# One buffer of keys and queries divided into four, in a sparse-attention and soft mixture-of-experts kernel

## Chip, cores and metric

The kernel runs on one core of one Trainium2 chip. The metric is the device time of one execution in microseconds (us). Before the change three runs gave a median of 304.71 us (303.28 to 306.85).

## What is computed

Inputs are q, k and v of 8 batches, 8 heads, 576 tokens and 64 values a head, all float32. The attention is sparse, its result is the input of a soft mixture of experts (MoE):

```python
scores = scale * np.matmul(q, k.transpose(0, 1, 3, 2))
mask_local = (rel >= 0) & (rel < stride)                      # stride 32, heads 0 to 3
mask_strided = (rel >= 0) & (pos[None, :] % stride == pos[:, None] % stride)   # heads 4 to 7
attn = softmax(where(mask, scores, -1e9));  attn_out = attn @ v
...
logits = x @ phi                  # x: 4608 tokens x 512, 32 slots
d = softmax(logits, axis=0);  slot_input = d.T @ x
slot_out[e] = relu(slot_input[e] @ w1[e]) @ w2[e]             # 8 experts, 4 slots each
out = softmax(logits, axis=1) @ slot_out
```

## The kernel before

The attention works in 16 groups (`i` = 0 to 15). A group is two local heads and two strided heads of one batch, so two groups make a batch; "even" and "odd" below mean `i`. The work of a group is cut into some 50 named steps, and a table `PHASE` gives each step a due time within a group. A step of group `i` is due at 10 · i + PHASE, all steps of all groups are sorted by that, and each engine runs its instructions in the order in which they were written. Semaphore waits are put in by the layer that records the instructions: it keeps track of who wrote and read what part of which buffer.

The steps that matter here, in the order of the data:

- `D` (lines 240 to 242): SyncE (SP) starts the load of 512 tokens of keys or queries of two heads, 256 KB, into one of three places of 512 columns (`nat`). `kL`, `qL`, `kS`, `qS` are local keys, local queries, strided keys, strided queries.
- `Dt` (lines 244 to 247), in even groups: SP starts two loads of 128 KB, the first 64 tokens of keys and of queries of all 8 heads of the batch, into the place `tnat`.
- `g` (lines 270 to 272): GpSimd (POOL) sorts a loaded place into one of two others (`nat2`).
- `T` (line 279) and `Tt` (line 300): TensorE (PE) transposes a sorted place, or `tnat`, into a PSUM bank (line 277).
- `e` (lines 282 to 297) and `et` (line 302): ScalarE (ACT) copies a bank into the transposed keys or queries `kt` or, for the first tokens, into `tl`. Keys take two copies of 64 rows, queries one of 128 rows.
- `kc` (lines 307 to 316): POOL copies keys of the first tokens from `tl` into `kt`.
- `SL` and `SS` (lines 321 to 337): PE computes the scores, 36 small products (`score`, line 319). `SL` writes a bank that the copies `ekS` had just emptied.
- `a`, `m`, `b`, `s` on VectorE (DVE), `EX` on ACT: mask, maximum, subtraction, exponential, sum (lines 347 to 369). `P`, `f`, `AA`, `AL`, `AS`, `n`, `X`, `LG` follow: weights transposed, values applied (line 397), normalised, transposed, logits. Every fourth group adds the steps of the 64 first tokens of a batch pair, and odd groups add the slot sums.
- `Dv`, `C2` (lines 249 to 268) and `Ds` (lines 257 to 262): loads and sorting of the values. `Ds` waits until PE has used the strided values of the group before.

Weights of the experts, 512 KB a load, go on the same SP queue between these loads: 28 into buffers of their own, spread over the attention, and 14 more into buffers of the attention (`alias`, lines 178 to 187) as each falls free near its end. After the last group PE, DVE and ACT compute the experts and the output (from line 651).

All places of keys and queries (`nat`, `nat2`, `kt`, `tl`, `tnat`) are column ranges of one buffer `kqn` of 6,912 columns: three places of `nat` at columns 0 to 1535, two of `nat2` at 1536 to 2559, then `kt` with kL (1,152 columns), qL (512), kS (1,152) and qS (512) up to 5887, `tl` at 5888 to 6399 and `tnat` at 6400 to 6911.

Of the kernel before, what the change touches and what calls it, by code (L numbers as in the profile page):

```python
# [19 lines left out]
B, H, S, D = 8, 8, 576, 64  # L20
# [13 lines left out]
    Tt=7.4853, et=9.1043, kcL=10.5339, kcS=12.0504, gkL=2.4513, gqL=2.5317, TkL=6.2817, ekL=8.2205, gkS=6.6666,  # L34
# [3 lines left out]
    AL=29.4276, AA=27.8312, nA=34.2734, nL=31.3378, AS=29.6166, nS=31.6162, XS=32.1661, xS=32.38, XL=31.9169,  # L38
# [35 lines left out]
def tile_sparse_attention_soft_moe(  # L74
# [23 lines left out]
    def big(nm, cols, dt=F32):  # L98
        return const.tile([P, cols], dt, name=nm)
# [12 lines left out]


    KQ = ("kL", "qL", "kS", "qS")
    kqn = big("kqn", 6912)
    pb = big("pb", 1152)
    ptb = big("ptb", 1024)
    vb_ = big("vb", 4096)
# [6 lines left out]
    def nat(x, i):  # L125

        lo = 512 * ((4 * i + KQ.index(x) + 2) % 3)
        return kqn[:, lo:lo + 512]

    def nat2(x):  # L130

        lo = 1536 + 512 * (KQ.index(x) % 2)
        return kqn[:, lo:lo + 512]

    kt, lo = {}, 2560
    for x in KQ:
        n = 2 * S if x[0] == "k" else S - 64
        kt[x] = kqn[:, lo:lo + n]  # L140
        lo += n
    tl = kqn[:, 5888:6400].rearrange("p (j x t) -> p j x t", j=4, x=2)
    tnat = kqn[:, 6400:6912]

    psg = {1: pb[:, 0:640].rearrange("p (s k a) -> p s k a", s=5, a=2),
           2: pb[:, 640:1152].rearrange("p (s x) -> p s x", s=4)[:, :, 0:3 * NI].rearrange("p s (k a) -> p s k a", a=3)[:, :, :, 0:2]}
# [25 lines left out]
    def give(t):  # L172
# [2 lines left out]

    alias = [(("gqL", "gkS", "gqS"), kqn, 0), (("gqS", "TkS", "TqS"), kqn, 1), (("TqS", "SL", "SS"), kqn, 2),
             (("SL", "SS"), kqn, 3), (("SL", "SS"), kqn, 4), (("SL", "SS", "kcS", "Tt-"), kqn, 5), (("AL-", "AA-", "C2-"), vb_, 0), (("AL", "AA", "C2"), vb_, 1), (("AL", "AA"), vb_, 2), (("AL", "AA"), vb_, 3),
             (("AS",), vs, 0), (("AS",), vs, 1), (("AS", "AL"), ptb, 0), (("LG", "XB"), xtb, 0)]  # L180

    def last(x):
        return PER * (NQ - 1 - x.count("-")) + PHASE[x.strip("-")]

    alias = sorted(((max(last(x) for x in names) + .01, n, t[:, 1024 * k:1024 * k + 1024]) for n, (names, t, k) in enumerate(alias)),
                   key=lambda x: x[:2])
# [53 lines left out]
    def emit_D(x, i):  # L240
        src = (k if x[0] == "k" else q)[i // 2, heads(i, x[1]), 64:]
        nc.sync.dma_start(out=nat(x, i).rearrange("p (h x) -> p h x", h=2), in_=src.rearrange("h (p n) d -> p h (n d)", n=TN))
# [27 lines left out]
    def emit_g(x, i):  # L270

        PC(out=nat2(x).rearrange("p (n h d) -> p h n d", n=TN, h=2), in_=nat(x, i).rearrange("p (h n d) -> p h n d", n=TN, h=2))  # L272
# [6 lines left out]
    def emit_T(x, i):  # L279
        turn("T" + x, i, nat2(x))  # L280
# [647 lines left out]
```

## Time and profile before

| what | us |
|---|---|
| runs before, median (lowest to highest) | 304.71 (303.28 to 306.85) |
| the profiled execution, own time | 302.76 |
| its span, first to last instruction | 301.0 |
| busy PE / DVE / ACT / POOL in the span | 235.7 / 182.5 / 154.7 / 101.2 |
| mean granted TensorE clock in the span | 0.924 |

The rows of the trace come from this one execution. PE is matrix products and transposes, PEld the loading of their stationary operand, SPq the queue of SP. "L296" is line 296 of the kernel. A number behind "idle before" or in square brackets is the time in which the engine did nothing ahead of the instruction, with what ended it. The granted clock is told as a share: 1.0 is 2.4 GHz and 0.5 is 1.2 GHz.

### The profile page before, as it was taken

What the parts mean: (1) busy time and instruction counts of PE and PEld (TensorE: products, weight loads), DVE (VectorE), ACT (ScalarE), POOL (GpSimd) and SP (SyncE); (2) the same over time, 40 slices, a digit from 0 to 9 for tenths busy, and PEclk for the clock granted to TensorE, in tenths of its full rate; (3) what the DMA queues carried; (4) which work ended last, traced back from release to release, by engine and by line L of the source; (5) the groups of instructions that cost most, each with busy time, mean ns of one, the idle gap of its engine ahead of it and who ended that gap; (6) DMA issues with size and microseconds to landing.
All of it is one profiled execution on the core that took longest, in us unless ns stands there. A gap on an engine that the chain in (4) does not pass through costs nothing.

```text
span 301.0 us, 9638 instructions
## 1 busy us (share of the span) xinstructions
PE 235.7 (78%) x3901; PEld 182.2 (61%) x3901; DVE 182.5 (61%) x405; ACT 154.7 (51%) x325; POOL 101.2 (34%) x170
## 2 busy tenths in 40 slices
PE   5866984994997897799699499992868977799800
PEld 2755973994977786788689497971632322355700
DVE  5063881684589588468689368993241466834720
ACT  1537735874664973777596467861210014524610
POOL 5473651653338258063466252621000200000000
PEclk9997996999899999799999799997777999999975
DMA  7999689579658868839696956499836999818997
GB/s 215 302 277 293 201 252 251 186 200 276 199 135 287 271 189 237 270 113 287 184 287 174 318 176 194 136 289 298 280 116 211 330 357 348 277 54 304 310 350 242
DMA packets 80940, 72.79 MB, mean 242 GB/s; under 512 B 33280, under 2 KB 75648, under 8 KB 80896
## 3 DMA queue, kind: packets, MB, share of 16 engines
q1 hardware_dynamic: 79936, 71.84, 78.4%
q8 instruction: 31, 0.51, 0.7%
q10 hardware_dynamic: 960, 0.33, 0.6%
q14 instruction: 13, 0.11, 0.1%
HBM read 62.72 MB, written 9.44 MB: 240 GB/s over the span
## 4 chain that ended last, share of the span: by engine, by line
PE 51%; DMA 19%; DVE 10%; ACT 9%; SPq 2%; issue 2%; POOL 1%; DVEq 0%; ACTq 0%; POOLq 0%
DMA kqn<-in_q_dram 14%; PE bank L319 9%; PE bank L277 8%; PE bank L397 6%; ACT kqn L296 6%; PE bank L839 4%; PE bank L871 3%; PE bank L736 3%; PE bank L442 3%; PE bank L566 3%; PE bank L389 3%; DMA vs<-in_v_dram 3%; DMA wb<-in_moe_w_dram 2%; PE bank L461 2%; PE bank L472 2%
## 5 line engine op out<-in xcount | busy, mean ns | idle before, releaser
L296 ACT COPY kqn<-bank 64x512 f32<-64x512 f32 (+1 forms) x96 | 59.2, 617 | 49.9 <-DMA kqn<-in_q_dram 40.6
L272 POOL COPY kqn<-kqn 128x512 f32<-128x512 f32 x64 | 41.7, 669 | 87.9 <-PE bank L277 45.6
L319 PE MATMUL bank<-kqn 128*32 128x128 f32 (+1 forms) x1152 | 36.9, 284 | 27.1 <-ACT kqn L296 27.1
L319 PEld LDWEIGHTS bank<-kqn 128*32 128x32 f32 x1152 | 32.9, 125 | 33.0 <-issue 20.1
L277 PE MATMUL bank<-cf,kqn 128*128 128x128 f32 x288 | 42.5, 297 | 4.0 <-POOL kqn L272 4.0
L277 PEld LDWEIGHTS bank<-cf,kqn 128*128 128x128 f32 x288 | 35.2, 153 | 9.3 <-POOL kqn L272 6.2
L354 DVE TENSOR_TENSOR pb<-bank,cb 128x512 f32<-128x512 f32 (+2 forms) x48 | 22.7, 474 | 29.3 <-PE bank L319 10.7
L424 DVE TENSOR_TENSOR xnb<-bank,rz 128x512 f32<-128x512 f32 x32 | 21.6, 687 | 11.6 <-PE bank L397 8.3
L369 DVE TENSOR_REDUCE rz<-pb 128x10 f32<-128x640 f32 (+1 forms) x32 | 21.9, 683 | 10.8 <-ACT pb L366 10.7
L362 DVE TENSOR_TENSOR pb<-pb,mx 128x640 f32<-128x640 f32 (+1 forms) x32 | 28.0, 875 | 0.6
L397 PE MATMUL bank<-vs,ptb 128*32 128x128 f32 x512 | 18.7, 282 | 5.8 <-DMA vs<-in_v_dram 5.8
L359 DVE TENSOR_REDUCE mx<-pb 128x10 f32<-128x640 f32 (+1 forms) x32 | 22.0, 688 | 0.6
L366 ACT ACTIVATE pb<-pb 128x640 f32<-128x640 f32 (+1 forms) x32 | 19.7, 615 | 1.8 <-DVE pb L362 1.7
L389 PE MATMUL bank<-cf,pb 128*128 128x128 f32 x128 | 20.1, 281 | 0.5 <-ACT pb L366 0.3
L393 ACT COPY ptb<-bank 128x512 f32<-128x512 f32 x32 | 19.4, 606 | 0.8 <-PE bank L389 0.8
L267 POOL COPY vb<-vb 64x1024 f32<-64x1024 f32 x16 | 16.6, 1037 | 8.5 <-DMA vb<-in_v_dram 7.5
L397 PEld LDWEIGHTS bank<-vs,ptb 128*32 128x32 f32 x512 | 15.5, 113 | 6.1 <-issue 6.1
L397 PE MATMUL bank<-vb,ptb 128*32 128x128 f32 x512 | 18.0, 274 | 0.0
L442 PE MATMUL bank<-cf,xnb 128*128 128x128 f32 x128 | 17.9, 284 | 0.1
L268 POOL COPY vb<-vb 64x1024 f32<-64x1024 f32 x16 | 17.0, 1060 | 0.7
L389 PEld LDWEIGHTS bank<-cf,pb 128*128 128x128 f32 x128 | 15.2, 145 | 1.7 <-ACT pb L366 0.9
L442 PEld LDWEIGHTS bank<-cf,xnb 128*128 128x128 f32 x128 | 14.8, 145 | 1.2 <-DVE xnb L424 0.7
(143 smaller groups left out, 375.3 us busy)
## 6 DMA issues: line engine op xcount, KB each, us to landing
wb<-in_moe_w_dram SPq DMA_DIRECT2D x47, 512.0 KB
kqn<-in_k_dram SPq DMA_DIRECT2D x32, 256.0 KB
kqn<-in_q_dram SPq DMA_DIRECT2D x32, 256.0 KB
vb<-in_v_dram SPq DMA_DIRECT2D x32, 144.0 KB
vs<-in_v_dram SPq DMA_DIRECT2D x32, 128.0 KB
kqn<-in_moe_w_dram SPq DMA_DIRECT2D x6, 512.0 KB
out_dram<-kqn SPq DMA_DIRECT2D x5, 512.0 KB
vb<-in_moe_w_dram SPq DMA_DIRECT2D x4, 512.0 KB
```

The lines of the kernel that those rows point to most:

```text
L272: PC(out=nat2(x).rearrange("p (n h d) -> p h n d", n=TN, h=2), in_=nat(x, i).rearrange("p (h n d) -> p h n d", n=TN, h=2))
L277: nc.tensor.transpose(out=t[0][:, 128 * n:128 * n + 128], in_=src[:, 128 * n:128 * n + 128], identity=ident)
L296: ACT(out=dst, in_=src)
L319: nc.tensor.matmul(out=t[0][32 * c:32 * c + 32, x:x + wd], lhsT=lhsT, rhs=rhs, start=True, stop=True, skip_group_check=True)
L354: nc.vector.tensor_tensor(out=dst, in0=box[t, i][0][:, lo:lo + 2 * n * kk].rearrange("p (s k a) -> p s k a", s=n, a=2), in1=mk.rearrange(" ...
L359: nc.vector.tensor_reduce(out=part(box[i][0], w), in_=psg[w].rearrange("p s k a -> p s a k"), op=ALU.max, axis=AX.X)
L362: nc.vector.tensor_tensor(out=psg[w], in0=psg[w], in1=over(box[i][0], w), op=ALU.subtract)
L369: nc.vector.tensor_reduce(out=part(box[i][1], w), in_=psg[w].rearrange("p s k a -> p s a k"), op=ALU.add, axis=AX.X)
L389: nc.tensor.transpose(out=t[0][:, 128 * r:128 * r + 128], in_=pb[:, lo + 128 * r:lo + 128 * r + 128], identity=ident)
L397: nc.tensor.matmul(out=t[0][32 * c:32 * c + 32, 128 * r:128 * r + 128], lhsT=lhsT, rhs=rhs, start=True, stop=True, skip_group_check=True)
L424: nc.vector.tensor_tensor(out=xn[:, place(i, s)].rearrange("p r (a d) -> p r a d", a=2), in0=t[0].rearrange("p (r a d) -> p r a d", r=4, a=2),
L442: nc.tensor.transpose(out=t[0][:, 128 * r:128 * r + 128], in_=xn[:, place(i, s), r, :], identity=ident)
```

## The change

The buffer `kqn` becomes four: `natb` (the loaded and sorted places and `tnat`), `kLb` (local keys), `kSb` (strided keys) and `qtb` (both queries and `tl`). They have 3,072 + 1,152 + 1,152 + 1,536 = 6,912 columns together. The list `alias`, which gives parts of 1,024 columns to expert weights at the end of the attention, is written for the new buffers: six parts as before, but two now lie in `natb` beyond the first, and each has its own last users. No computation, size or due time is changed. From the line of the buffers on the numbers of lines move, at most by one behind line 176.

```diff
-    kqn = big("kqn", 6912)
+    natb = big("natb", 3072)
+    kLb, kSb = big("kLb", 2 * S), big("kSb", 2 * S)
+    qtb = big("qtb", 1536)
...
-        return kqn[:, lo:lo + 512]
+        return natb[:, lo:lo + 512]
...
-    kt, lo = {}, 2560
-    for x in KQ:
-        n = 2 * S if x[0] == "k" else S - 64
-        kt[x] = kqn[:, lo:lo + n]
-        lo += n
-    tl = kqn[:, 5888:6400].rearrange("p (j x t) -> p j x t", j=4, x=2)
-    tnat = kqn[:, 6400:6912]
+    kt = {"kL": kLb, "kS": kSb, "qL": qtb[:, 0:512], "qS": qtb[:, 512:1024]}
+    tl = qtb[:, 1024:1536].rearrange("p (j x t) -> p j x t", j=4, x=2)
+    tnat = natb[:, 2560:3072]
...
-    alias = [(("gqL", "gkS", "gqS"), kqn, 0), (("gqS", "TkS", "TqS"), kqn, 1), (("TqS", "SL", "SS"), kqn, 2),
-             (("SL", "SS"), kqn, 3), (("SL", "SS"), kqn, 4), (("SL", "SS", "kcS", "Tt-"), kqn, 5), (("AL-", "AA-", "C2-"), vb_, 0), (("AL", "AA", "C2"), vb_, 1), (("AL", "AA"), vb_, 2), (("AL", "AA"), vb_, 3),
+    alias = [(("gqL", "gkS", "gqS"), natb, 0), (("gqS", "TkS", "TqS"), natb, 1), (("TqS", "Tt-"), natb, 2),
+             (("SL", "SS"), kLb, 0), (("SL", "SS"), kSb, 0), (("SL", "SS"), qtb, 0),
+             (("AL-", "AA-", "C2-"), vb_, 0), (("AL", "AA", "C2"), vb_, 1), (("AL", "AA"), vb_, 2), (("AL", "AA"), vb_, 3),
```

What it does to the instructions is seen in the waits. On ACT the copies of group 5 stand like this before; the first two rows are the copies of its strided keys (`ekS`), the third of its strided queries. Names with HW are the semaphores of transfers, eight of which the SP queue uses in turn:

```order
L296 COPY kqn<-bank_120 64x16x32 [waits DMAHW0_49,DMAHW7_49,PE_49,Activation_49]
L296 COPY kqn<-bank_120 64x16x32 [waits Activation_49]
L296 COPY kqn<-bank_114 128x512 [waits PE_49,Activation_49]
L446 COPY xtb<-bank_115 128x512 [waits PE_49,Activation_49]
L452 COPY xtb<-bank_119 128x512 [waits DVE_49,PE_49]
```

The same place of the changed kernel:

```order
L295 COPY kSb<-bank_123 64x16x32 [waits PE_49,Activation_49]
L295 COPY kSb<-bank_123 64x16x32 [waits Activation_49]
L295 COPY qtb<-bank_117 128x512 [waits PE_49,Activation_49]
L445 COPY xtb<-bank_118 128x512 [waits PE_49,Activation_49]
L451 COPY xtb<-bank_122 128x512 [waits DVE_49,PE_49]
```

The first copy no longer waits for two transfers; nothing else moved. The two are the `Dt` loads of group 6, whose `tnat` lies in other columns than the strided keys. The same pair of waits goes from the `ekS` copies of groups 1, 3, 5, 7, 9, 11 and 13, and in group 0 from the copies of the local keys; group 15 has none.

On the SP queue the two `Dt` loads (line 247) of group 6 stand here before, between the loads of local queries and of strided keys:

```order
L242 DMA kqn<-in_q_dram 128x2x256 [waits DMAHW6_49,Pool_49]
L247 DMA kqn<-in_k_dram 64x8x64 [waits DMAHW7_49,Activation_49]
L247 DMA kqn<-in_q_dram 64x8x64 [waits DMAHW0_49]
L242 DMA kqn<-in_k_dram 128x2x256 [waits DMAHW1_49,Pool_49]
L261 DMA vs<-in_v_dram 32x1024 [waits DMAHW2_49,PE_49]
```

And in the changed kernel:

```order
L241 DMA natb<-in_q_dram 128x2x256 [waits DMAHW6_49,Pool_49]
L246 DMA natb<-in_k_dram 64x8x64 [waits DMAHW7_49]
L246 DMA natb<-in_q_dram 64x8x64 [waits DMAHW0_49]
L241 DMA natb<-in_k_dram 128x2x256 [waits DMAHW1_49,Pool_49]
L260 DMA vs<-in_v_dram 32x1024 [waits DMAHW2_49,PE_49]
```

The first `Dt` load no longer waits for a copy of ACT, in group 6 that of the local queries of group 5; in group 0 a wait for DVE goes, in group 2 it becomes one for PE, and the others lose theirs. The third place is the end of the attention on the SP queue. Before, one weight load stands ahead of the values `Dv` of group 15 (line 252) and four behind:

```order
L216 DMA kqn<-in_moe_w_dram 128x4x256 [waits DMAHW3_49,PE_49,Pool_49]
L252 DMA vb<-in_v_dram 64x9x64 [waits DMAHW4_49]
L252 DMA vb<-in_v_dram 64x9x64 [waits DMAHW5_49]
L216 DMA kqn<-in_moe_w_dram 128x4x256 [waits PE_49,DMAHW6_49,Activation_49,Pool_49]
L216 DMA kqn<-in_moe_w_dram 128x4x256 [waits DMAHW7_49,Activation_49]
```

After:

```order
L215 DMA natb<-in_moe_w_dram 128x4x256 [waits DMAHW3_49,PE_49,Pool_49]
L215 DMA natb<-in_moe_w_dram 128x4x256 [waits DMAHW4_49,PE_49]
L251 DMA vb<-in_v_dram 64x9x64 [waits DMAHW5_49]
L251 DMA vb<-in_v_dram 64x9x64 [waits DMAHW6_49]
L215 DMA kLb<-in_moe_w_dram 128x4x256 [waits PE_49,DMAHW7_49,Activation_49,Pool_49]
```

One weight load of 512 KB has moved ahead of the values. The order on PE, ACT, DVE and POOL is the same in both kernels.

## Rows read from the trace of the kernel before

**Rows 1.** The waits of all engines: who waited, for whom, us in total, times, longest.

```profile
ACT kqn L296 <- DMA kqn<-in_q_dram: 40.6, 8, 7.9
...
PE bank L319 <- ACT kqn L296: 27.1, 7, 5.6
```

**Rows 2.** Timeline around the wait of group 5: start, length, engine, instructions, idle time before.

```profile
66.14 0.75 ACT L366 ACTIVATE pb<-pb 128x640 f32<-128x640 f32 x1
66.89 1.09 PE L277 MATMUL bank<-cf,kqn 128*128 128x128 f32 x8
66.95 0.63 SPq L247 DMA_DIRECT2D kqn<-in_q_dram  x1
72.01 1.83 ACT L296 COPY kqn<-bank 64x512 f32<-64x512 f32 x3 [5.12 <-DMA kqn<-in_q_dram]
73.37 1.93 PE L319 MATMUL bank<-kqn 128*32 128x128 f32 x53 [3.96 <-ACT kqn L296]
```

**Rows 3.** The chain that ended last, in order of time: start, us, what.

```profile
41.40 6.64 DMA kqn<-in_q_dram
...
66.95 4.91 DMA kqn<-in_q_dram
```

**Rows 4.** Windows: length, busy PE, PEld, DVE, ACT, POOL (instructions), granted clock, DMA share, GB/s.

```profile
60.70:69.40 8.70, 8.70 (x202) 7.96 (x193) 7.78 (x15) 4.89 (x11) 5.02 (x9) 1.00 0.80 223
69.40:73.40 4.00, 0.04 (x5) 0.06 (x5) 1.42 (x4) 1.34 (x3) 1.22 (x2) 1.00 0.81 231
73.40:87.00 13.60, 13.60 (x240) 12.16 (x244) 8.91 (x21) 10.49 (x24) 5.51 (x10) 0.87 0.59 179
87.00:96.30 9.30, 9.27 (x199) 7.96 (x190) 8.07 (x17) 5.06 (x11) 4.92 (x9) 1.00 0.90 269
96.30:99.20 2.90, 0.01 (x2) 0.04 (x3) 1.30 (x4) 1.32 (x3) 1.17 (x2) 1.00 0.68 196
99.20:109.70 10.50, 10.50 (x226) 9.39 (x230) 7.87 (x17) 9.61 (x21) 6.28 (x10) 1.00 0.78 253
109.70:118.20 8.50, 8.48 (x197) 7.77 (x189) 8.34 (x17) 5.08 (x11) 5.01 (x10) 1.00 0.79 223
118.20:122.00 3.80, 0.00 (x0) 0.01 (x1) 1.45 (x4) 1.28 (x3) 1.22 (x2) 1.00 0.70 186
...
183.90:193.10 9.20, 9.20 (x199) 8.16 (x191) 7.98 (x17) 6.83 (x15) 4.86 (x8) 1.00 0.63 189
```

**Rows 5.** Longer windows of the attention, and one short one.

```profile
0.00:24.00 24.00, 16.18 (x160) 11.06 (x160) 9.72 (x18) 8.53 (x14) 14.20 (x27) 1.00 0.92 268
24.00:48.00 24.00, 18.40 (x370) 16.66 (x370) 15.29 (x30) 13.41 (x27) 11.71 (x20) 0.91 0.82 244
48.00:194.00 146.00, 127.12 (x2535) 113.67 (x2539) 105.42 (x223) 101.02 (x211) 70.17 (x118) 0.95 0.74 219
66.00:72.00 6.00, 3.41 (x57) 2.97 (x49) 4.37 (x7) 0.89 (x2) 4.15 (x8) 1.00 0.95 294
```

**Rows 6.** The SP queue's own waits.

```profile
SPq L247 <- DVE kqn L617: 1.6, 1, 1.6
```

**Rows 7.** Timeline of SP and POOL: loads of keys and queries and their sorting.

```profile
60.13 0.37 SPq L242 DMA_DIRECT2D kqn<-in_q_dram  x1
...
64.74 0.38 SPq L242 DMA_DIRECT2D kqn<-in_k_dram  x1
...
69.84 0.61 POOL L272 COPY kqn<-kqn 128x512 f32<-128x512 f32 x1 [0.64 <-DMA kqn<-in_k_dram]
...
71.48 0.38 SPq L242 DMA_DIRECT2D kqn<-in_q_dram  x1
```

**Rows 8.** Timeline of POOL and PE at the end of the attention.

```profile
200.52 1.03 POOL L267 COPY vb<-vb 64x1024 f32<-64x1024 f32 x1 [7.47 <-DMA vb<-in_v_dram]
...
203.68 1.06 PE L397 MATMUL bank<-vb,ptb 128*32 128x128 f32 x32
...
210.58 1.93 PE L397 MATMUL bank<-vs,ptb 128*32 128x128 f32 x32 [5.84 <-DMA vs<-in_v_dram]
```

More of the change, by code (lines that the diff above doesn't have):

```diff
@@ L127, in nat @@
         lo = 512 * ((4 * i + KQ.index(x) + 2) % 3)
-        return kqn[:, lo:lo + 512]
+        return natb[:, lo:lo + 512]
     def nat2(x):
         lo = 1536 + 512 * (KQ.index(x) % 2)
-        return kqn[:, lo:lo + 512]
-    kt, lo = {}, 2560
-    for x in KQ:
-        n = 2 * S if x[0] == "k" else S - 64
-        kt[x] = kqn[:, lo:lo + n]
-        lo += n
-    tl = kqn[:, 5888:6400].rearrange("p (j x t) -> p j x t", j=4, x=2)
-    tnat = kqn[:, 6400:6912]
+        return natb[:, lo:lo + 512]
+    kt = {"kL": kLb, "kS": kSb, "qL": qtb[:, 0:512], "qS": qtb[:, 512:1024]}
+    tl = qtb[:, 1024:1536].rearrange("p (j x t) -> p j x t", j=4, x=2)
+    tnat = natb[:, 2560:3072]
     psg = {1: pb[:, 0:640].rearrange("p (s k a) -> p s k a", s=5, a=2),
```

## The prediction

> **What bounds the kernel now.** I read the table of waits first, then the timeline around its longest entries, the chain that ended last, and windows cut at the ends of the waits. In the table the reader is to see one wait that leads to another: ACT stood 40.6 us in 8 waits before a copy of line 296, each until a load of queries had landed, and PE stood 27.1 us in 7 waits before the scores, line 319, until such a copy was done [rows 1]. The timeline shows one of them whole. In group 5 ACT was free at 66.89 (66.14 + 0.75). PE began the transposes of strided keys and queries there and ended them at 67.98. Yet the copy of the strided keys began at 72.01, after 5.12 us [rows 2]. What landed then was started at 66.95 by line 247, that is `Dt`, the first tokens of group 6: in the chain that load takes 4.91 us, to 71.86 [rows 2, 3]. The copy neither reads nor writes what it brings. PE could not begin the scores of group 5 before the copy had emptied their bank, and began at 73.37, after 3.96 us of idleness [rows 2].
>
> The windows show what the kernel is bound by apart from that. From 60.7 to 69.4 PE is busy for 8.70 of 8.70 us, then 0.04 of 4.00; from 73.4 to 87.0 all of 13.60; 9.27 of 9.30, then 0.01 of 2.90; 10.50 of 10.50; 8.48 of 8.50, then 0.00 of 3.80 [rows 4]. Between the waits PE leaves no gap, in them it does nothing, and this repeats every second group.
>
> **The change part by part.**
>
> *The wait of ACT for `Dt`.* It goes from the copies of groups 1, 3, 5, 7, 9, 11 and 13. What is late next is in group 5 the end of the transposes: the two copies of keys, 0.6 us each, can begin at about 67.5 and end at 68.7, and PE comes to the scores at 69.4. So PE's whole idle time goes: 7 waits, 27.1 us [rows 1]. The trace has a case without the wait. Group 15 has no `Dt` behind it, and the stretch 183.9 to 193.1 that leads to it took 9.20 us, where its like, 87.0 to 99.2, took 9.30 + 2.90 = 12.20 [rows 4]. The difference, 3.0 us, is the idle time. In group 0 the wait ended when PE's transposes ended as well, so I count nothing.
>
> *What DVE takes back.* In the waits DVE worked on: 1.42, 1.30 and 1.45 us [rows 4]. With the stretch before, it has 7.78 + 1.42 = 9.20 us of work where PE has 8.70, 9.37 where PE has 9.30, and 9.79 where PE has 8.50. That is 0.5, 0.07 and 1.3 us more, 0.6 in the mean, and the next copies hang on DVE's results through the exponential. Seven times 0.6 is 4.3 us back. The other groups have 8.91 of DVE in 13.60 and hide it [rows 4]. Bounds: 0 if DVE uses its slack there, 9 if all seven are like the third.
>
> *What the transfers take back.* The bytes stay, so the DMA engines must go faster. In the first 48 us they were busy 0.92 · 24 + 0.82 · 24 = 41.8 us [rows 5]. The best share that a row shows is 0.95 [rows 5]; at that, they need 44.0 us. PE's first two idle times lie there; the longest is 5.6 [rows 1], and with one like the others they are 9.5. Only 4 of these fit if every byte is wanted by then, so 5.5 come back; none do if the loads there run ahead of their use. I take 3, the middle. In the rest the share is 0.74 over 146 us, 108 us of work [rows 5]. Less the other five idle times, about 17.5 us, that is 108 in 128.5, a share of 0.84. I charge nothing for it, and the rival below does.
>
> *The clock.* The granted clock was 0.91 from 24 to 48 us and 0.95 from 48 to 194 [rows 5], 0.09 · 24 + 0.05 · 146 = 9.5 us of lost clock. It fell to half in some stretches that follow a wait: 0.87 from 73.4 to 87.0 after 4.0 us without products, but 1.00 from 99.2 to 109.7 after 2.9 [rows 4]. Without these waits between 0 and 9.5 us return. I take 3, since a faster PE then meets DVE, with 35.4 us of work in the four groups from 60.7 to 109.7 [rows 4].
>
> The Trainium skill, in TensorE: Matmul & The Clock Gate, section HAM oscillation, says that a wait for DMA in every round lets the clock fall, that the work behind it then starts at half speed, and that this costs the throttled time times one half. By that rule all of the 9.5 us would return. The trace agrees in one of the two cases above and not in the other.
>
> *The wait of SP ahead of `Dt`.* In group 0 it was for DVE, 1.6 us [rows 6]. The next loads go out that much earlier, but the DMA engines are at a share of 0.92 there [rows 5], so between 0 and 1.6 us is won; I take 1. The other seven held SP until ACT's copy of local queries. They go too, and the loads behind (strided keys, values) start earlier. Nothing of this costs time, and it is part of the slack that the transfers need.
>
> *The weight load ahead of `Dv` of group 15.* 512 KB at 294 GB/s [rows 5] are 1.8 us. The values come that much later, so POOL's sorting at 200.52 and PE's products at 203.68 too. They have cover: the next products wait until 210.58 for the other values, 5.84 us [rows 8], and the bytes ahead of those stay the same. I count nothing; without the cover it costs 1.8.
>
> *The rest.* No instruction is added or changed, and the four memsets of the key buffers stay four.
>
> The sum: -27.1 + 4.3 + 3 - 3 - 1 = -23.8 us. Against the profiled execution's own 302.76 that is 279.0. The median of the runs shown is 1.95 above it, so I predict 280.9 for the median. The term bounds give -27.1 - 9.5 - 1.6 = -38.2 on one side and -27.1 + 9 + 5.5 = -12.6 on the other.
>
> **The rivals.**
>
> *The loads become the bound.* A place for loaded keys is free only when POOL has sorted it, and SP stands until then. From the load of strided queries at 60.13 to the next at 71.48 is 11.35 us, and 5.1 of them lie between the start of a load at 64.74 and POOL's sorting at 69.84 [rows 7]. For it: the loads already take 4.9 and 6.6 us in the chain [rows 3], and at a higher share they would wait longer for each other. Against it: SP issued nearly without pause in that time, and from 99.2 to 109.7 PE ran without a gap at a share of 0.78 [rows 4]. If each group took 11.35 us, a pair would take 22.7, where four groups from 73.4 to 122.0 took 48.6, 24.3 a pair [rows 4]. Then 1.6 · 7 = 11 us are won: 293.5 to the median.
>
> *All of the clock returns, and DVE keeps up.* Then -27.1 + 2 + 1 - 8 - 1 = -33: 271.7. For it: PE has no gap between waits, so each microsecond at half speed shows in full. Against it: DVE has 8.34 us of work in a window of 8.50 [rows 4].
>
> *Slower: the end of the attention waits for transfers.* Its place is the wait for the last values, 210.58 [rows 8]. Until 194 us the transfers have 22.1 + 19.7 + 108.0 = 149.8 us of work [rows 5]. If they could not pass the mean share of 149.8 / 194 = 0.77, everything won would be spent again there. The moved weight load would add 1.8 us, and a half clock behind the longer wait what it cost from 73.4 to 87.0, 0.13 · 13.6 = 1.8 [rows 4]: 304.71 + 3.6 = 308.3. It decides from the point where the share cannot rise above 0.77; rows 5 show 0.92 over 24 us, so I think it unlikely.
>
> *The change does not do what it says.* The layer that records the instructions could have put other waits in their place. The order shows none in the attention, so this is as unlikely: 304.7.
>
> **How the numbers follow.** Forecast 0.60, the loads 0.17, the clock 0.19, slower 0.02, no effect 0.02. The forecast's own range is 275 to 288. The range reaches towards the two larger rivals, 270 to 293, and leaves some 0.15 out. A measurement of this kernel can tell about 1% from no change; 293.5 is still 3.7% faster, so faster has 0.96, within 1% 0.02, slower 0.02.
>
> **What would show it.** Right: the wait of ACT for the load of queries is gone from the table, and PE's idle time before line 319 is under 6 us in total; windows of odd groups last 8.5 to 10 us without an idle piece behind; the granted clock is 1.0 from 50 us to the end of the attention; the share of DMA in the attention is above 0.80; the time between the end of the attention and the end of the program has not changed by more than 2 us. The terms would be wrong if PE is idle before its transposes or POOL before line 272 until a load has landed (the loads), or if PE waits for DVE or ACT ahead of line 389 (DVE). The prediction is wrong if PE's idle time only moves to another line.

## The result, and the profile after

The changed kernel takes 277.34 us in the median of 4 executions (276.10 to 278.78), the kernel before 304.94 beside it: a ratio of 0.9095, 95% interval 0.9025 to 0.9165. Two more sessions, told among the experiments, gave 0.9179 and 0.9131. Ratios and intervals leave out executions that lie well above the fastest of their kernel; medians count all. The profiled execution took 277.12, with a span of 275.3 (before 302.76 and 301.0) and a mean granted clock of 0.942 (before 0.924).

The waits of the changed kernel, all engines and then PE's own: who waited, for whom, us in total, times, longest.

```profile
POOL natb L271 <- DMA natb<-in_q_dram: 23.5, 18, 4.1
POOL natb L271 <- DMA natb<-in_k_dram: 22.7, 15, 3.5
...
PE bank L276 <- POOL natb L271: 12.1, 12, 2.3
PE bank L396 <- DMA vs<-in_v_dram: 6.0, 3, 4.8
...
PE bank L276 <- DVE pb L361: 0.7, 1, 0.7
```

Both waits of [rows 1] are gone: no copy of ACT waits for a load, and PE has no wait before its scores (now line 318). In their place PE waits before its transposes (276) for POOL's sorting (271), and POOL for loaded keys and queries. From the first transposes to the last wait for values, at 181.5, one wait of PE is for DVE, of 0.7 us, and none for ACT. A part of the wait for POOL stood in the kernel before already:

```profile
PE bank L277 <- POOL kqn L272: 4.0, 5, 1.8
```

The timeline at the place of [rows 2], group 5:

```profile
60.31 1.09 PE L276 MATMUL bank<-cf,natb 128*128 128x128 f32 x8
...
61.05 1.30 ACT L295 COPY kSb<-bank 64x512 f32<-64x512 f32 x2 [0.77 <-PE bank L276]
...
62.75 1.18 PE L318 MATMUL bank<-kLb,qtb 128*32 128x128 f32 x34
```

The copies of strided keys now begin 0.74 us after PE began the transposes that feed them, where they began 5.12 us behind (72.01 against 66.89), and the scores have no idle time ahead (no bracket).

Three windows divide the span: up to the last wait for values, that wait, and the rest. The columns are those of [rows 4]. Before:

```profile
0.00:204.74 204.74, 172.07 (x3295) 149.57 (x3295) 140.86 (x296) 130.12 (x268) 98.27 (x167) 0.95 0.78 231
204.74:210.58 5.84, 0.00 (x1) 0.03 (x2) 1.03 (x3) 0.00 (x0) 1.06 (x1) 0.73 1.09 275
210.58:301.00 90.42, 63.61 (x606) 32.59 (x606) 40.57 (x107) 24.54 (x57) 1.84 (x2) 0.88 0.82 265
```

After:

```profile
0.00:181.52 181.52, 166.08 (x3295) 142.28 (x3295) 137.06 (x297) 131.17 (x268) 96.65 (x168) 0.97 0.90 261
181.52:186.63 5.11, 0.26 (x9) 0.29 (x12) 0.69 (x1) 0.00 (x0) 0.16 (x1) 0.85 1.08 279
186.63:275.30 88.67, 62.35 (x606) 32.28 (x598) 40.59 (x107) 24.61 (x57) 1.84 (x2) 0.88 0.84 271
```

The same 3295 products stand in the first window. Of its 23.2 us, PE's idle time gave 17.2 (204.74 - 172.07 = 32.7, then 181.52 - 166.08 = 15.4) and PE's busy time 6.0. The wait for values gave 0.7 and the rest 1.8; together 25.7, the difference of the spans. The 17.2 are two things: the 27.1 of [rows 1] went, and 9.9 came back. Of these, 8.1 are the longer wait for POOL before the transposes (12.1 against 4.0), 0.7 the wait for DVE, and most of the rest short waits for strided values.

Windows of the attention after the change show where:

```profile
0.00:24.00 24.00, 17.76 (x212) 12.55 (x216) 12.45 (x25) 12.40 (x22) 13.64 (x27) 0.86 0.92 269
24.00:48.00 24.00, 19.24 (x386) 17.09 (x390) 14.33 (x30) 15.71 (x32) 11.99 (x21) 0.94 0.88 259
48.00:96.00 48.00, 46.39 (x971) 40.91 (x964) 37.87 (x83) 37.14 (x78) 27.46 (x47) 0.99 0.91 263
96.00:144.00 48.00, 47.15 (x1032) 41.96 (x1025) 41.03 (x92) 38.80 (x81) 25.93 (x47) 1.00 0.89 257
```

Of the 15.4 us of idle time, 11.0 lie in the first 48 us (48 - 17.76 - 19.24). From 48 to 144 us PE is busy for 97% to 98%, at a clock of 0.99 to 1.00, with the DMA engines at a share of about 0.9 where they stood at 0.74 [rows 5].

### The profile page after: what moved, and what is told of

Same layout as the page of the kernel before. It is cut to its first block, busy times and chain, and to the rows that moved or that the text cites. A ratio compares the mean times of both kernels' runs of the same rounds, so it can differ in the third digit from the quotient of the medians.

```text
span 275.3 us, 9626 instructions
## 1 busy us (share of the span) xinstructions
PE 228.7 (83%) x3901; PEld 174.9 (64%) x3901; DVE 178.3 (65%) x405; ACT 155.8 (57%) x325; POOL 98.7 (36%) x170
## 4 chain that ended last, share of the span: by engine, by line
PE 49%; DMA 21%; DVE 11%; POOL 5%; SPq 4%; issue 3%; ACT 2%; DVEq 0%; POOLq 0%; ACTq 0%
DMA natb<-in_q_dram 14%; PE bank L276 8%; PE bank L396 7%; PE bank L318 4%; PE bank L838 4%; PE bank L441 4%; DMA natb<-in_k_dram 4%; PE bank L870 4%; POOL natb L271 3%; PE bank L735 3%; PE bank L388 2%; PE bank L565 2%; DMA vs<-in_v_dram 2%; PE bank L471 2%; DVE ct L811 2%
## 5 line engine op out<-in xcount | busy, mean ns | idle before, releaser
L271 POOL COPY natb<-natb 128x512 f32<-128x512 f32 x64 | 40.8, 641 | 70.8 <-DMA natb<-in_q_dram 23.5
L276 PE MATMUL bank<-cf,natb 128*128 128x128 f32 x288 | 43.2, 293 | 12.9 <-POOL natb L271 12.1
L276 PEld LDWEIGHTS bank<-cf,natb 128*128 128x128 f32 x288 | 33.5, 148 | 21.0 <-POOL natb L271 17.0
L295 ACT COPY kSb<-bank 64x512 f32<-64x512 f32 x32 | 20.2, 631 | 11.4 <-PE bank L276 11.0
L295 ACT COPY kLb<-bank 64x512 f32<-64x512 f32 x32 | 20.5, 640 | 9.5 <-PE bank L276 9.0
L361 DVE TENSOR_TENSOR pb<-pb,mx 128x640 f32<-128x640 f32 (+1 forms) x32 | 25.2, 787 | 0.6
L318 PE MATMUL bank<-kLb,qtb 128*32 128x128 f32 x576 | 22.3, 283 | 0.0
L318 PEld LDWEIGHTS bank<-kLb,qtb 128*32 128x32 f32 x576 | 18.0, 113 | 4.1 <-issue 2.4
L295 ACT COPY qtb<-bank 128x512 f32<-128x512 f32 x32 | 18.8, 589 | 2.1 <-PE bank L276 1.7
L388 PE MATMUL bank<-cf,pb 128*128 128x128 f32 x128 | 19.3, 273 | 0.0
```

The source lines that it names most:

```text
L276: nc.tensor.transpose(out=t[0][:, 128 * n:128 * n + 128], in_=src[:, 128 * n:128 * n + 128], identity=ident)
L295: ACT(out=dst, in_=src)
L318: nc.tensor.matmul(out=t[0][32 * c:32 * c + 32, x:x + wd], lhsT=lhsT, rhs=rhs, start=True, stop=True, skip_group_check=True)
L361: nc.vector.tensor_tensor(out=psg[w], in0=psg[w], in1=over(box[i][0], w), op=ALU.subtract)
L388: nc.tensor.transpose(out=t[0][:, 128 * r:128 * r + 128], in_=pb[:, lo + 128 * r:lo + 128 * r + 128], identity=ident)
```

## The experiments

Twelve runs in three sessions; the ratios are to executions of the kernel before in the same session (medians 305.02, 305.94 and 305.16 us). The theory was that ACT's false wait for `Dt` is the whole cause, and that what remains of PE's idle time is the full DMA engines. The diffs are cut: where `tnat` or a place of `natb` moves, its size and the list `alias` move with it.

**The first tokens alone.** Of the kernel before, only `tnat` leaves the buffer:

```diff
-    kqn = big("kqn", 6912)
+    kqn = big("kqn", 6400)
+    tnat = big("tnb", 512)
...
-    tnat = kqn[:, 6400:6912]
```

> The kernel before with one edit: the place of the first tokens (tnat) gets a buffer of its own, and keys, queries and natural places stay in the one large buffer. Theory (the whole gain is that ACT's copies no longer wait for the load Dt into that buffer): the time of the changed kernel, 275 to 280 us, and the wait of ACT for the load of queries is gone from the table (40.6 us before). Rival (the other splits, keys from queries and natural from sorted, carry part of the gain): in between, 285 to 298 us, with ACT or SP still waiting for something in that buffer.

280.41 us, ratio 0.9162 [0.9111, 0.9214]. The waits:

```profile
POOL kqn L272 <- DMA kqn<-in_q_dram: 25.2, 21, 4.5
ACT kqn L296 <- PE bank L277: 23.2, 21, 2.5
```

ACT's copies now wait for PE's transposes alone, and the loads have the same new place in the table as in the changed kernel. The interval overlaps all three of the changed kernel: two buffers do what four do.

**The first tokens with the strided keys.** Four buffers, but with the one tie put back:

```diff
-    kLb, kSb = big("kLb", 2 * S), big("kSb", 2 * S)
+    kLb, kSx = big("kLb", 2 * S), big("kSb", 2 * S + 512)
+    kSb = kSx[:, 0:2 * S]
...
-    tnat = natb[:, 2560:3072]
+    tnat = kSx[:, 1152:1664]
```

> The four buffers of the change, with one edit: tnat lies in the buffer of the strided keys, which ACT copies into in every second group. Theory (ACT's wait for Dt is the cause): the time of the kernel before comes back, 298 to 306 us, with some 7 idle times of PE before the scores, 24 to 30 us in the table. Rival (the split into four is worth something by itself, whoever shares with tnat): 277 to 292 us.

A ratio of 1.0034 [0.9965, 1.0102] (medians 308.81 and 305.02). The waits:

```profile
ACT kSb L296 <- DMA kSb<-in_q_dram: 41.9, 7, 8.0
POOL kSb L316 <- DMA kSb<-in_q_dram: 41.5, 7, 8.0
...
PE bank L319 <- ACT kSb L296: 27.5, 6, 6.3
```

The two rows of [rows 1] stand there again, 41.9 and 27.5 us, with the buffer's new name. POOL's copies of first tokens into that buffer wait too. This kernel has one place fewer for weights at the end of the attention, so its whole time is not quite that of one edit; the waits inside the attention are what counts. So the split into four is worth nothing by itself; who shares with `tnat` decides.

**The first tokens with the queries.** It keeps SP's wait and takes ACT's wait from the copies of strided keys:

```diff
-    qtb = big("qtb", 1536)
+    qtb = big("qtb", 2048)
...
-    tnat = natb[:, 2560:3072]
+    tnat = qtb[:, 1536:2048]
```

> The four buffers of the change, with one edit: tnat lies in the buffer of the transposed queries. SP then still waits for ACT's copies of local queries before it issues Dt, as before the change, but ACT's copies of strided keys do not wait for Dt. It tells the two removed waits apart. Theory (SP's wait is covered): 276 to 281 us, at most 2 us more than the changed kernel. Rival (a good part of the gain is that SP issues the loads behind Dt earlier): 283 to 295 us, and the waits of POOL for natural keys and queries are longer by as much.

280.60 us, ratio 0.9133 [0.9052, 0.9214], as the theory has it. The SP queue still waits for ACT there, but for 2.0 us in all. The wait of group 0 for DVE [rows 6] is gone here as well, so this run does not price it:

```profile
SPq L246 <- ACT kSb L295: 1.0, 2, 0.6
SPq L246 <- ACT pb L365: 1.0, 1, 1.0
```

**The weight load moved back.**

```diff
-(("TqS", "Tt-"), natb, 2)
+(("TqS", "SL", "SS"), natb, 2)
```

> The changed kernel with one edit: the third place of the natural buffer is given to the weights where the kernel before gave it, so that the moved weight load stands behind the values of group 15 again. Theory (the moved load is covered): the time of the changed kernel within 1 us, 276 to 279. Rival (the 1.8 us by which the last values come later are paid at the end of the attention): 274 to 276 us, with the wait of PE for the last values 1 to 2 us shorter.

281.10 us, ratio 0.9155 [0.9077, 0.9233]. It lies 3.8 us above the time first measured for the changed kernel, but only 0.5 to 0.7 above the other two kernels of its session, so I took the changed kernel along in the next two.

> The changed kernel once more, beside the next runs, since kernels that should equal it came out 1% above it in another session. Either 276 to 279 us again (then those 1% are theirs), or 279 to 281 (then they are the session's).

280.97 us, ratio 0.9179 [0.912, 0.9238].

> The changed kernel beside the next runs, as the measure for them: 276 to 281 us.

280.26 us, ratio 0.9131 [0.903, 0.9231]. So the 1% was the session's, and the rival of the moved load, 274 to 276 us, did not come: the load costs nothing that can be measured. The changed kernel is worth 8% to 9% in all three sessions.

**The 28 spread weight loads at the end of the attention.**

```diff
-        tasks.append((PHASE["Dw"] + (alias[0][0] - PHASE["Dw"]) * w / NWBUF, "w", w))
+        tasks.append((alias[0][0] - 0.5 + 0.01 * w, "w", w))
```

> The changed kernel with the 28 loads of weights all issued at the end of the attention instead of being spread over it. Theory (in the attention PE now waits before its transposes because the DMA engines are full): these waits, 12.1 us for POOL in the changed kernel, fall to under 5 us and the attention ends 5 to 10 us earlier than 181.5. Rival (the wait is the order of places and of SP's queue, not the bytes): the waits stay above 9 us and the attention ends within 2 us of 181.5. The whole time is no test: the weights are wanted behind the attention, and it may be longer, 275 to 295.

297.86 us in all (ratio 0.9709 [0.9649, 0.9769]), since the last values now stand behind the weights. The attention is what counts here. Windows, and the row of PE's waits:

```profile
24.00:48.00 24.00, 23.59 (x515) 21.34 (x513) 20.33 (x43) 19.53 (x41) 15.50 (x28) 1.00 0.71 200
48.00:96.00 48.00, 48.00 (x1041) 43.25 (x1040) 42.97 (x90) 40.42 (x84) 29.26 (x50) 1.00 0.71 194
...
PE bank L276 <- POOL natb L271: 3.2, 6, 0.8
```

With these weights out of the way PE's wait for POOL falls from 12.1 to 3.2 us. In the second 24 us PE gets 515 products done, where the changed kernel has 386 and the kernel before 370 [rows 5]. The late values hide where the attention would have ended, so I compare a step shortly before: the exponentials of the strided weights of group 14 come 14.4 us earlier, in the timelines of this kernel and of the changed one:

```profile
156.34 0.49 ACT L365 ACTIVATE pb<-pb 128x288 f32<-128x288 f32 x1
```

```profile
170.76 0.52 ACT L365 ACTIVATE pb<-pb 128x288 f32<-128x288 f32 x1
```

That is more than the 5 to 10 us that I had expected. The run takes the 28 loads off SP's queue as well as their bytes off the DMA engines. That the bytes count is seen in the time of one load after its start. In the chain of the changed kernel that ended last, ten loads of keys and queries take 2.87 to 6.84 us each. In this run the median of all 32 loads of queries, from issue to landing (the last number), is 3.0. A chain picks late loads, so this is a sign and no proof:

```profile
33.51 2.87 DMA natb<-in_q_dram
...
132.95 6.84 DMA natb<-in_q_dram
```

```profile
natb<-in_q_dram SPq DMA_DIRECT2D x32, 256.0 KB, 3.0
```

What fewer loads on SP's queue give by themselves was not tried. And where the loads are on time PE is busy for 48.00 of 48.00 us, with DVE at 42.97: DVE does not bound the attention.

**Four places for loaded keys and queries.**

```diff
-    natb = big("natb", 3072)
+    natb = big("natb", 3584)
...
-        lo = 512 * ((4 * i + KQ.index(x) + 2) % 3)
+        lo = 512 * KQ.index(x)
```

> The changed kernel with four places for loaded keys and queries instead of three, one for each of the four of a group, so that each load may go out one load earlier. Theory (the DMA engines are full): little, 0 to 3 us less than the changed kernel. Rival (the lack of places makes the loads late): 4 to 9 us less, 268 to 273, with the wait of PE for POOL before the transposes under 5 us.

275.55 us, ratio 0.9004 [0.8942, 0.9067], beside 0.9179 for the changed kernel in the same session: 5.4 us less. First windows, and PE's waits:

```profile
0.00:24.00 24.00, 18.10 (x214) 12.34 (x218) 12.40 (x25) 12.61 (x22) 14.32 (x28) 0.86 0.98 288
24.00:48.00 24.00, 20.96 (x475) 18.60 (x470) 16.27 (x35) 17.61 (x36) 13.54 (x25) 1.00 0.96 265
...
PE bank L276 <- POOL natb L271: 10.0, 13, 2.2
PE bank L396 <- DMA vs<-in_v_dram: 5.5, 1, 5.5
```

Each side has half of it. The gain lies in the rival's 4 to 9 us (the time itself does not lie in its 268 to 273, which counted from 277), and the share of 0.98 and 0.96 in the first 48 us (0.92 and 0.88 with three places) shows that the lack of places had kept the engines from being full there. But PE's wait for POOL is still 10.0 us, not under 5: with the places there the loads still come late, and the run before points to their bytes. As `alias` changed, the 28 weight loads also fall due some 3% earlier; that was not told apart.

**The last values ahead of the weights.** In PE's waits with four places, one of 5.5 us remains at the end of the attention. The SP queue's timeline of that kernel shows why: four weight loads are issued just ahead of the last values.

```profile
170.89 0.51 SPq L215 DMA_DIRECT2D kLb<-in_moe_w_dram  x1
171.57 0.38 SPq L215 DMA_DIRECT2D kSb<-in_moe_w_dram  x1
172.07 0.59 SPq L215 DMA_DIRECT2D qtb<-in_moe_w_dram  x1
172.78 0.43 SPq L215 DMA_DIRECT2D vb<-in_moe_w_dram  x1
173.30 0.80 SPq L260 DMA_DIRECT2D vs<-in_v_dram  x1
```

One line added to the kernel with four places gives these four, and one into `natb` ahead of them, a later due time:

```diff
+    alias = [(max(x[0], last("Ds") + .01) if n > 1 else x[0],) + x[1:] for n, x in enumerate(alias)]
     order = wbufs + [t for _, _, t in alias]
```

> Four places for loaded keys and queries, and in addition the loads of weights into the last place but one of the natural buffer, the keys', the queries' and the first of the values' buffer stand behind the strided values of group 15 instead of ahead of them (5 loads, 2.5 MB). Theory (the wait of PE at the end of the attention, 5.26 us with four places, is for values queued behind these bytes, and the engines have room for them afterwards): the wait falls under 1.5 us and the time by 3 to 5 us against four places alone, 270 to 272.5. Rival (the weights behind are late in their turn): the wait goes, but comes back in the part behind the attention, 274 to 277 us.

269.43 us, ratio 0.885 [0.8782, 0.8918], beside 0.9131 for the changed kernel. SP and PE in its timeline:

```profile
173.57 0.61 SPq L262 DMA_DIRECT2D vs<-in_v_dram  x1
174.22 0.44 SPq L216 DMA_DIRECT2D natb<-in_moe_w_dram  x1
...
177.46 1.06 PE L397 MATMUL bank<-vb,ptb 128*32 128x128 f32 x32
178.34 1.06 PE L397 MATMUL bank<-vs,ptb 128*32 128x128 f32 x32
```

The products with the last values follow those before them with no idle time, and the weights were in time. The ratio is 0.0154 under that of four places alone, 4.7 us, as expected, though in another session. The version is 11% to 12% under the kernel before.

**All seven such loads later.**

```diff
+    alias = [(max(x[0], last("Ds") + .01),) + x[1:] for x in alias]
```

> As the kernel before this one, and all 7 loads of weights into buffers of the attention, with the 28 loads ahead of them spread over the whole attention up to there: 3.5 MB fewer in it. Theory (in the attention PE still waits for loads since the engines are full): 1 to 3 us less than the kernel before this one, 267 to 271. Rival (weights late behind the attention): 272 us or more.

269.65 us, ratio 0.8794 [0.8665, 0.8923]. It can't be told from the kernel before it, so the 1 to 3 us expected are not shown.

**The clock by itself, first try.** In the kernel before, 24 products into unread columns:

```diff
+        if i % 2 and i < NQ - 1:
+            for n in range(24):
+                nc.tensor.transpose(out=t[0][:, 128:256], in_=pb[:, 512:640], identity=ident)
```

> The kernel before, with 24 products more that nobody reads in every odd group but the last, set into the time in which PE waits before the scores. The waits stay; PE is not idle in them. It measures the term of the clock by itself. Theory (the half-speed stretches behind the waits cost time): 4 to 6 us less than before, 299 to 301, with the granted clock of the attention at 0.98 or more. Rival (a faster PE behind the wait only waits for DVE, or the fall of the clock has another cause): within 1.5 us of before, and the clock as it was, or high and without effect.

313.36 us, ratio 1.022 [1.0148, 1.0293]: neither. The products of an odd group run well behind its wait: in group 5 PE stands idle from 73.2 to 75.5, and the products come at 87.66. The last row is all 168 of them, with their busy time:

```profile
73.20:75.50 2.30, 0.00 (x0) 0.00 (x0) 1.37 (x4) 1.26 (x3) 1.08 (x2) 0.99 0.67 217
...
87.66 2.78 PE L380 MATMUL bank<-cf,pb 128*128 128x128 f32 x24
...
L380 PE MATMUL bank<-cf,pb 128*128 128x128 f32 x168 | 19.5, 273 | 0.0
```

The run was no test of the clock; it shows that where PE does not wait, part of the added work is paid: 7.4 of 19.5 us (313.36 against 305.94).

**The clock by itself, second try.** The same products in the even groups, right ahead of the seven idle times:

```diff
+        if i % 2 == 0 and i < NQ - 2:
```

> The kernel before, with 24 products more that nobody reads behind the last products ahead of each of the seven idle times of PE (the even groups 0 to 12; the run with them in the odd groups had them one group too late, where they lay on the path). They take about 2.8 us of the 4 us in which PE waits. The waits stay as they are. Theory (the half-speed stretches that follow the waits cost time, the seven waits caused 5 to 6 us of it): 3 to 6 us less than before, 299 to 302, with the granted clock of the attention at 0.98 or more. Rival (it is worth nothing, as a faster PE then meets DVE or the loads, or the clock falls for another reason): within 1.5 us of before.

The median is 299.22 us, 5.9 under the 305.16 beside it. The interval of the ratio, 0.9684 [0.9577, 0.979], says 6.4 to 12.9 us less; the smaller figure is the surer one. Its windows, the last up to the wait for the last values:

```profile
0.00:48.00 48.00, 38.38 (x578) 31.77 (x578) 25.35 (x48) 21.92 (x40) 24.46 (x45) 0.96 0.85 251
48.00:194.00 146.00, 138.30 (x2747) 124.69 (x2751) 108.36 (x231) 103.47 (x216) 73.13 (x120) 0.99 0.76 225
0.00:202.00 202.00, 184.01 (x3463) 161.80 (x3463) 141.48 (x297) 130.11 (x268) 99.97 (x168) 0.98 0.79 235
```

The granted clock is 0.99 from 48 to 194 us, where it was 0.95 [rows 5]: 0.04 · 146 = 5.8 us. The 3463 products are the 3295 of the kernel before and the 168 added, which take 19.5 us here too. So the 3295 took 184.01 - 19.5 = 164.5 us, 7.5 less than before (172.07). The profiled execution gains only 2.8 of it (299.95 against 302.76), since the added products do not all fit into the waits. The gain is at the upper end of what I had expected, or above it. The rival falls: a kernel that does more work, with the false waits in place, is faster, because the engine that waited did not rest.

## Why the prediction was right, and where its terms were not

The time predicted for the median, 280.9 us, lies at the upper end of the three sessions' 277.3 to 281.0, and the mechanism is the one named. The two largest errors among the terms had opposite signs, so the sum came out better than its parts.

*The wait of ACT for `Dt`, -27.1.* Right. The runs with `tnat` alone and with `tnat` beside the strided keys show it as the whole cause, from both sides. Why the layer that records the instructions counts two separate column ranges of one buffer as touching was not tried; that another buffer ends it was.

*What DVE takes back, +4.3.* Wrong: 0.7, near its lower bound. The step that failed is "the next copies hang on DVE's results": DVE had 7.78 + 1.42 us of work per 8.70 of PE, but PE waited for it once. In the run with late weights PE runs 48.00 of 48.00 us with DVE at 42.97.

*What the transfers take back, +3.* Wrong in size: 9.2 (9.9 without the wait for DVE), above its bound of 5.5. Two steps failed. The first was that the engines could go to 0.95 in the first 48 us; they stayed at 0.92 and 0.88, since SP stood without a free place, and reached 0.98 and 0.96 only with a fourth. The second was to charge nothing behind 48 us, where a share of 0.84 was to do; the share became about 0.9, and 15.4 - 11.0 = 4.4 us of idle time lie there, the 0.7 for DVE among them. The mechanism is that of the rival in which the loads become the bound, and the sign named for it was seen: POOL idle before line 271 until a load has landed. Its price, 11.35 us a group, was too high.

*The clock, -3.* Right in sign, too small: PE's busy time for the same 3295 products fell by 6.0 us, and by 7.5 in the second try. In the changed kernel a part stays lost. Windows of that kernel:

```profile
7.60:14.40 6.80, 6.33 (x64) 5.15 (x68) 0.32 (x1) 2.90 (x5) 3.43 (x9) 0.50 1.01 332
27.20:29.50 2.30, 0.02 (x1) 0.00 (x0) 2.25 (x6) 1.21 (x2) 0.63 (x2) 1.00 1.09 298
29.50:36.00 6.50, 6.46 (x137) 6.03 (x141) 3.28 (x8) 4.66 (x10) 4.83 (x9) 1.00 0.70 222
43.00:45.10 2.10, 0.01 (x2) 0.01 (x1) 1.54 (x4) 0.68 (x2) 0.99 (x2) 1.00 1.09 286
45.20:48.60 3.40, 3.40 (x28) 3.01 (x32) 0.00 (x0) 1.88 (x4) 1.21 (x3) 0.50 0.82 202
```

PE worked at half of its full clock (1.2 instead of 2.4 GHz) from 45.2 to 48.6, behind 2.1 us of idleness, and at the full clock behind 2.3 us at 27.2. The two stretches at 0.50 cost about half of 6.8 + 3.4, so 5.1 us. The first of them seems not to be new. In the kernel before, eight transposes took as long there as eight at 10.18 take in the changed kernel, 1.97 us, where eight took 1.09 at a granted clock of 1.00 [rows 2, 4]:

```profile
10.44 1.97 PE L277 MATMUL bank<-cf,kqn 128*128 128x128 f32 x8 [0.81 <-POOL kqn L272]
```

The granted clock of that window is told as 1.00 [rows 5], so the 9.5 us of the prediction are probably less than the kernel before lost.

By the rule weighed in the prediction (the Trainium skill, TensorE: Matmul & The Clock Gate, section HAM oscillation: a wait for DMA lets the clock fall and the work behind it starts cold) all 9.5 us would have returned. The trace has 6.0, and 7.5 in the second try; that a wait is followed by a fall each time is not what these rows show.

*SP's wait, -1.* Not shown: the term is the wait of group 0 for DVE, and no run sets it apart. The waits for ACT are worth nothing that can be measured: the run that keeps them has a ratio of 0.9133.

*The weight load ahead of `Dv`, 0.* Right, by the run that moves it back.

*Not in the sum.* The last wait for values became 0.7 us shorter and the part behind it 1.8. With them the measured terms are -27.1 + 0.7 + 9.2 - 6.0 + 0 - 0.7 - 1.8 = -25.7, where the prediction had -23.8. Its sign that the time behind the attention changes by no more than 2 us holds for that part alone (1.8) and is missed with the last wait (2.5).

## What to carry to other kernels

When a wait in the table names a transfer that the waiting instruction doesn't read, look at which buffer the two share, and move only that place: here one place of 512 columns in a buffer of its own was worth as much as the split into four. Before counting the idle time as won, look at the loads of that time: their share, and the free places that their queue needs; the 9.9 us that they took back were the largest correction, and a fourth place and a better order of the last loads won about as much again. An engine's idle time costs more than its length where the clock falls behind it.

## What the runs showed of the hardware that was not expected

Products that nobody reads, 168 in number, made the kernel before 2.1% to 4.2% faster by the interval, 1.9% by the medians, when they filled PE's waits, with the granted clock going from 0.95 to 0.99, and the same number one group away made it 1.5% to 2.9% slower. The fall of the clock does not follow from the length of one wait alone: 2.1 us of idleness were followed by a clock of 0.50 and 2.3 us by 1.00 in the same execution, and in the kernel before 2.9 us by 1.00 [rows 4]. And over 24 us the DMA engines held a share of 0.98 with four places, where the kernel before had 0.92 at best [rows 5].
